# Half-size products with sums of operands in the output projection of a fused attention and feed-forward kernel

## The chip, the cores and the metric

The kernel runs on one core of a Trainium2 chip. The metric is the device time of one execution in microseconds, the median of several runs. The engines are named as the profile names them: PE (TensorE, matrix products; PEld its weight loads), DVE (VectorE), ACT (ScalarE), POOL (GpSimd) and SP (SyncE, which here only issues DMA transfers). Results of PE land in PSUM, eight banks of 512 fp32 values per partition. In this kernel PSUM is emptied by VectorE and ScalarE, while GpSimd works only on operands in SBUF.

## The reference

Attention in which two neighbouring queries are averaged first, then a feed-forward part without a nonlinearity:

```python
def _attn_ref(q, k, v):                      # (8, 8, 1152, 64) each
    q_pool = q.reshape(B, H, S // 2, 2, D).mean(axis=3)
    scores = scale * np.matmul(q_pool, k.transpose(0, 1, 3, 2))
    scores = scores - np.max(scores, axis=-1, keepdims=True)
    attn = np.exp(scores)
    attn = attn / (np.sum(attn, axis=-1, keepdims=True) + 1e-09)
    return np.matmul(attn, v)

def _moe_ref(x, w1, w2, w3, w_out):          # x: 4608 tokens of 512
    a = x @ w1
    b = x @ w2
    h = a * b @ w3
    return h @ w_out
```

## The kernel before

The products with `w3` and `w_out` are folded: `T = w3 @ w_out` (1024 x 512, fp16, `T16`) is made once on the chip, so for each token the rest is `a = x w1`, `b = x w2`, the gate `g = a * b` and `g T`.

**Attention.** The 64 heads are worked as 32 pairs. The key-query plane of all pairs is cut into 324 slots of 512 columns. For each slot PE computes the scores of both heads into a two-bank PSUM tile (`scores`, L431), and ScalarE takes the exponential into a ring in SBUF (L436). Three slots are one visit; there are 108. AV groups (`av_mm`, L459 and L462) multiply the exponentials with V into the bank `avb`, VectorE divides by the sums (`av_norm`, L483, L488, L497), and the result is turned into `xT`, by PE (`x_turn`, L504, L507, with copies L515, L517) or by a DMA transpose (`x_dma`, L473).

**Preparing the pairs.** At the first slot of pair n, `prepare(n + 2)` puts on GpSimd's queue the casts of K and Q of pair n + 2 (`cast_kq`: L343, L347, L349) and of V of pair n + 1 (`cast_v`: L356), and queues the loads of later pairs on SP (for the first eight pairs on GpSimd). K and Q of pair n + 1 are transposed at that place, for the first pairs on PE (L371), later by DMA from SP's queue (`transp`, L363). Each engine's queue is in order.

**Feed-forward.** 4608 tokens are nine chunks of 512. `moe_groups(c)` yields the groups of a chunk: for each of eight `ft` (128 of the 1024 hidden columns) one group of four 512-wide matmuls with `w1` (`first`, copied to `asb` by `keep`) and one with `w2` (`gate`: VectorE multiplies the PSUM result with `asb` into the fp16 tile `g`), then for each 128 tokens one group of eight 512-wide matmuls of `g` with `T16` (L610). `put` scales that result by VectorE into `osb` (L620) and `store` writes 128 rows; in attention the store goes over GpSimd's queue. T itself is made by `t_groups`: transposes of w3 (L535), then groups of eight 256-wide matmuls (L544).

**The order.** These groups are fills for PE between scores and AV groups. `_visits` plans before launch, by a model of PE, ScalarE and VectorE (`_Plan`, with a cost of 1 for a group of four 512-wide matmuls or eight 256-wide ones and 2 for one of eight 512-wide ones), which fills and AV groups each visit holds and whether a fill takes the single bank `mo` or one of the three `psc` tiles of the scores (`mot` in the profile). The plan doesn't have GpSimd in it. After the last slot the rest of the AV groups and fills follow; from there on `tail[0]` is true, ScalarE copies `asb` (L593), shares the emptying of outputs (L616, L617), and the stores go over SP and ScalarE. The last group of the last chunk is cut into 384 and 128 columns (`go_last`, L628). At the end a count of rows whose softmax sums left their range is read, and a general version runs if there are any (`near` sets where in the last chunk that read stands).

Of the kernel before, what the change touches and what calls it, by code (L numbers as in the profile page):

```python
# [8 lines left out]
FP32 = mybir.dt.float32  # L9
# [112 lines left out]
class _Plan:  # L122
# [39 lines left out]
        self.act = max(self.act, self.t + 0.21) + 0.953  # L162
        self._put(b, self.act + 0.07)

    def fill(self, n, at, scored):
        if scored:
            b = self._psc()
            self._pe("full", max(at, self.psc[b]), self.STEP[n])
            self._put(b, self._dve(0.2, 0.69))
        else:  # L170
            self._pe("full", max(at, self.mo), self.STEP[n])
            self.mo = self._dve(0.2, 0.69)

    def av_group(self, turns, last):
        self._pe("col" if last else "full", self.av, last * self.LAST if last else self.AV)
# [15 lines left out]
def _visits(n, start, units, pairs, fills, free, ready, width):  # L191

    p = _Plan(7.0)
    for _ in range(3):
        p.scores(0.0)
    beam = {(0, 0): [p]}
    for vis in range(n):  # L200
        new = {}
        ats = pairs.get(vis, [])

        def end(p, seq, na, f):
            q = p.copy()
            for _ in range(3 if vis + 1 < n else 0):
                q.scores(ready[vis + 1])
            q.past = (p.past, seq)

            cost = q.lost() + 0.3 * max(q.av - q.t, 0.0) + 0.15 * max(q.mo - q.t, 0.0)  # L210
            new.setdefault((na, f), []).append((cost, seq, q))

        def step(p, seq, na, f, pr, t0):
            d = p.t - t0
            loose = free[na] if vis >= start else 0
            if pr == len(ats) and (na >= len(units) or units[na][3] > vis) and (d > 1.0 or f >= loose):
                end(p, seq, na, f)
            if d > 2.3 or len(seq) > 4:
                return
            if pr < len(ats):  # L220
                q = p.copy()
                q.pair(ats[pr])
                step(q, seq + "P", na, f, pr + 1, t0)
            if na < len(units) and units[na][2] <= vis and seq.count("A") < 3:
                q = p.copy()
                q.av_group(*units[na][:2])
                step(q, seq + "A", na + 1, f, pr, t0)
            if f < loose:
                for b in "ms":
                    q = p.copy()  # L230
                    q.fill(fills[f][0], fills[f][1], b == "s")
# [24 lines left out]
def kernel(  # L256
# [26 lines left out]
    QM = 4  # L283
# [29 lines left out]
    wosb = msb.tile([128, NF, dm], FP16)  # L313
# [213 lines left out]
    def t_groups():  # L527
        w3T = {}

        def turn(ft):  # L530
            def go(pt):
                w3T[ft] = msb.tile([128, NF, 128], FP16, tag="w3T", bufs=2, name="w3T")
                ph = pt.bitcast(FP16)
                for a in range(NF):
                    nc.tensor.transpose(ph[:, a * 128:a * 128 + 128],  # L535
                                        w3c[ft // 4][:, ft % 4, a * 128:a * 128 + 128], ident16)

            return 0.5, go, lambda pt: nc.vector.tensor_copy(out=w3T[ft].rearrange("p a i -> p (a i)"),
                                                             in_=pt.bitcast(FP16)), W3_AT[ft // 2]

        def mult(ft, n0):
            def go(pT):
                for a in range(NF):
                    nc.tensor.matmul(pT[:, 0:256], w3T[ft][:, a, :], wosb[:, a, n0:n0 + 256],  # L544
                                     start=(a == 0), stop=(a == NF - 1))

            return 1, go, lambda pT: nc.vector.tensor_copy(out=T16[:, ft, n0:n0 + 256], in_=pT[:, 0:256]), WO_AT

        for ft in range(0, NF, 2):
            yield turn(ft)  # L550
            yield turn(ft + 1)
            for n in range(4):
                yield mult(ft + n // 2, n % 2 * 256)

    CH = 512

# [25 lines left out]
    def moe_groups(c):  # L582
        t = {}

        def first(pa, ft):
            if ft == 0:
                t["g"] = msb.tile([128, NF, CH], FP16, tag="g8", bufs=2, name="gT")
            proj(pa, w1sb, ft, c)

        def keep(pa):  # L590
            t["a"] = msb.tile([128, CH], FP32, tag="asb", bufs=2, name="asb")
# [11 lines left out]
        tts = list(range(0, CH, 128))  # L603
        if c in final:
            tts.sort(key=lambda tt: (c * CH + tt) % (2 * Sq) != QM * 128)
        for n, tt in enumerate(tts):
            def go(po, tt=tt, n=n):
                near[0] = c in final and n >= len(tts) - 3
                for ft in range(NF):
                    nc.tensor.matmul(po, t["g"][:, ft, tt:tt + 128], T16[:, ft, :],  # L610
                                     start=(ft == 0), stop=(ft == NF - 1))

            def put(po, tt=tt):
                osb = msb.tile([128, dm], FP32, tag="osb", bufs=3)
                if tail[0]:
                    nc.vector.tensor_scalar_mul(out=osb[:, 0:256], in0=po[:, 0:256], scalar1=1.0 / (SCL * SCL))  # L616
                    nc.scalar.mul(out=osb[:, 256:512], in_=po[:, 256:512], mul=1.0 / (SCL * SCL))  # L617
                    store(nc.scalar if c in final and tt == tts[-2] else nc.sync, c * CH + tt, osb)
                else:
                    nc.vector.tensor_scalar_mul(out=osb, in0=po, scalar1=1.0 / (SCL * SCL))  # L620
                    store(nc.gpsimd, c * CH + tt, osb)

            def go_last(po, tt=tt):
                osb = msb.tile([128, dm], FP32, tag="osb", bufs=3)
                for hs in (slice(0, 384), slice(384, dm)):
                    ph = ps.tile([128, 2, 512], FP32, tag="psc", bufs=3, name="mol")[:, 0, 0:hs.stop - hs.start]
                    for ft in range(NF):
                        nc.tensor.matmul(ph, t["g"][:, ft, tt:tt + 128], T16[:, ft, hs],  # L628
                                         start=(ft == 0), stop=(ft == NF - 1))
                    if hs.start:  # L630
                        nc.scalar.mul(out=osb[:, hs], in_=ph, mul=1.0 / (SCL * SCL))
                    else:
                        nc.vector.tensor_scalar_mul(out=osb[:, hs], in0=ph, scalar1=1.0 / (SCL * SCL))
                store(nc.scalar, c * CH + tt, osb)

            if c in final and n == len(tts) - 1:
                yield 2, go_last, None, 0.0
            else:
                yield 2, go, put, 0.0

    queue, ahead = [], []

# [94 lines left out]
                      ((old * FLAT + RING + TO[t]) // G) // VS - 1))  # L737
    fills = []
    for ft in range(0, NF, 2):
        fills += [(0.5, W3_AT[ft // 2])] * 2 + [(1, WO_AT)] * 4  # L740
# [71 lines left out]

    NQ = NU * 2
    rzf = rzall.rearrange("p i u -> p (i u)")
    ok = const.tile([128, 2, NQ], FP32)
# [53 lines left out]
```

## Time and profile before

| | us |
|---|---|
| median of 3 runs | 415.91 |
| lowest, highest | 415.29, 417.45 |
| the profiled execution's span | 414.1 |
| busy: PE, ScalarE, VectorE, GpSimd | 399.9, 323.4, 205.5, 167.6 |
| output groups (L610, L628), PE busy | 45.6 + 19.6 + 2.1 |
| feed-forward groups with w1 and w2 (L566), PE busy | 41.1 + 38.0 + 36.2 + 33.1 |

The span goes from the first to the last instruction of one profiled execution; its busy times are not times of the other runs. Matmuls overlap in the pipeline, so the mean time of one (380 ns for 512 columns) is longer than the spacing of two (216 ns). ScalarE's exponentials run from 8 to 348 us; the six output phases of chunks 0 to 5 lie at 100, 147, 190, 234, 277 and 323 us, and three chunks are finished after the last exponential.

### The profile page before, as it was taken

To read this page: it belongs to the slowest core of one execution; us is meant where nothing else is said; L and a number is where in the kernel's file an instruction comes from. 1 tells how busy PE (TensorE), PEld (TensorE's weight loads), DVE (VectorE), ACT (ScalarE), POOL (GpSimd) and SP (SyncE) were. 2 spreads that over 40 slices of the span, in tenths; PEclk is the share of its full clock that TensorE was granted. 3 is DMA by queue.
4 is the path that set the end of the run, shared out by engine and by line. 5 is a ranking of instruction groups with operands and counts; after the bars stand their busy time and mean duration, and the time that the engine had idled before them with its cause. 6 is when DMAs were issued, how large, how long until landed. Compare 5 with 4: busy or idle time off the path is not lost.

```text
span 414.1 us, 12744 instructions
## 1 busy us (share of the span) xinstructions
PE 399.9 (97%) x5337; PEld 246.9 (60%) x5337; DVE 205.5 (50%) x573; ACT 323.4 (78%) x353; POOL 167.6 (40%) x212
## 2 busy tenths in 40 slices
PE   3899999999999999999999999999999999999995
PEld 1477787565556655566556556655777655644442
DVE  1256665665356535554455436553556346744241
ACT  4878979898989998899999999999899986022321
POOL 4979976470655316504535155505532210010000
PEclk9999999999999999999999999999999999999999
DMA  8999999999799898959999999998975440030302
GB/s 263 210 320 289 269 286 312 348 247 265 185 238 252 221 286 278 242 70 278 273 264 280 264 252 270 292 260 163 303 207 121 85 90 15 16 114 2 101 0 108
DMA packets 90832, 86.34 MB, mean 209 GB/s; under 512 B 59664, under 2 KB 64272, under 8 KB 90768
## 3 DMA queue, kind: packets, MB, share of 16 engines
q1 hardware_dynamic: 81312, 58.80, 59.1%
q0 software_dynamic: 8880, 25.63, 21.6%
q10 hardware_dynamic: 576, 1.05, 0.8%
q8 instruction: 42, 0.69, 0.7%
q14 instruction: 22, 0.18, 0.1%
HBM read 67.11 MB, written 9.44 MB: 185 GB/s over the span
## 4 chain that ended last, share of the span: by engine, by line
PE 93%; ACT 2%; DMA 2%; DVE 1%; issue 1%; SPq 0%; POOL 0%; ACTq 0%
PE psc L431 20%; PE avb L462 17%; PE mot L566 16%; PE mo L566 15%; PE mo L610 11%; PE mot L610 5%; PE mo L544 3%; PE avb L459 3%; ACT ring L436 2%; PE ptk L371 2%; DMA kst<-in_k_dram 2%; DVE kqT L373 1%; PE mot L544 1%; PE mo L535 1%; PE mot L535 1%
## 5 line engine op out<-in xcount | busy, mean ns | idle before, releaser
L436 ACT ACTIVATE ring<-psc 128x1024 f16<-128x1024 f32 x324 | 308.3, 1025 | 33.8 <-PE psc L431 32.0
L462 PEld LDWEIGHTS <-ring 128*128 128x128 f16 x2304 | 84.4, 98 | 26.3 <-issue 7.1
L431 PE MATMUL psc<-kqT 64*128 64x512 f16 (+7 forms) x1152 | 96.2, 291 | 3.4 <-ACT ring L436 0.9
L462 PE MATMUL avb<-vaug,ring 128*128 128x65 f16 x2304 | 91.4, 193 | 0.0
L343 POOL CAST kq<-kst 128x1152 f16<-128x1152 f32 x31 | 35.7, 1150 | 74.3 <-DMA kqT<-kq 52.3
L431 PEld LDWEIGHTS <-kqT 64*128 64x128 f16 x1152 | 46.0, 95 | 31.0 <-issue 8.4
L578 POOL DMA_DIRECT2D out_dram<-osb x23 | 12.7, 551 | 101.6 <-DVE rzall L483 99.9
L610 PE MATMUL mo<-T,gT 128*128 128x512 f16 x192 | 45.6, 380 | 0.0
L566 PEld LDWEIGHTS <-w2sb 128*128 128x128 f16 x320 | 28.2, 98 | 28.3 <-issue 4.2
L566 PEld LDWEIGHTS <-w1sb 128*128 128x128 f16 x320 | 28.2, 98 | 27.7 <-issue 3.9
L610 PEld LDWEIGHTS <-gT 128*128 128x128 f16 x280 | 25.3, 98 | 32.2 <-issue 5.2
L483 DVE RECIPROCAL rzall<-avb 128x2 f32<-128x2 f32 x144 | 23.8, 165 | 37.0 <-PE avb L462 20.2
L566 PE MATMUL mot<-xT,w1sb 128*128 128x512 f16 (+2 forms) x172 | 41.1, 364 | 0.1
L620 DVE TENSOR_SCALAR osb<-mo 128x512 f32<-128x512 f32 x24 | 16.6, 692 | 48.5 <-PE mo L610 48.5
L347 POOL TENSOR_TENSOR kq<-qst 128x512 f16<-128x512 f32 x31 | 39.4, 1272 | 1.2 <-DMA qst<-in_q_dram 1.2
L566 PE MATMUL mot<-xT,w2sb 128*128 128x512 f16 (+2 forms) x156 | 38.0, 368 | 0.0
L356 POOL CAST vaug<-vst 128x1152 f16<-128x1152 f32 x32 | 36.6, 1143 | 2.6 <-DMA vst<-in_v_dram 2.5
L599 DVE TENSOR_TENSOR gT<-mot,asb 128x512 f16<-128x512 f32 x37 | 25.6, 692 | 22.0 <-PE mot L566 20.8
L599 DVE TENSOR_TENSOR gT<-mo,asb 128x512 f16<-128x512 f32 x35 | 24.2, 692 | 24.6 <-PE mo L566 24.4
L566 PE MATMUL mo<-xT,w2sb 128*128 128x512 f16 (+2 forms) x164 | 36.2, 349 | 0.0
L595 DVE COPY asb<-mo 128x512 f32<-128x512 f32 x32 | 22.1, 691 | 24.0 <-PE mo L566 23.7
L566 PE MATMUL mo<-xT,w1sb 128*128 128x512 f16 (+2 forms) x148 | 33.1, 351 | 0.0
(76 smaller groups left out, 287.4 us busy)
## 6 DMA issues: line engine op xcount, KB each, us to landing
vst<-in_v_dram SPq DMA_DIRECT2D x25, 576.0 KB, 4.9
kst<-in_k_dram SPq DMA_DIRECT2D x23, 576.0 KB, 5.9
qst<-in_q_dram SPq DMA_DIRECT2D x23, 512.0 KB, 7.2
out_dram<-osb POOLq DMA_DIRECT2D x23, 256.0 KB, 5.2
kst<-in_k_dram POOLq DMA_DIRECT2D x8, 576.0 KB, 9.8
qst<-in_q_dram POOLq DMA_DIRECT2D x8, 512.0 KB, 10.4
vst<-in_v_dram POOLq DMA_DIRECT2D x7, 576.0 KB, 7.2
w3c<-in_moe_w_dram POOLq DMA_DIRECT2D x4, 512.0 KB, 8.1
```

Of the source, the lines that this page charges most:

```text
L343: nc.gpsimd.tensor_copy(out=kq16[:, 0:NJ].rearrange("p c u d -> p u c d"), in_=kst.rearrange("p u (c d) -> p u c d", d=D))
L347: eng.tensor_tensor(out=kq16[:, NJ:NJ + QM].rearrange("p c u d -> p u c d"), in0=qv[:, :, :, 0], in1=qv[:, :, :, 1], op=ALU.add)
L356: nc.gpsimd.tensor_copy(out=va[:, :, :, 0:D], in_=vs.pop(p).rearrange("p u (c d) -> p u c d", d=D))
L431: nc.tensor.matmul(psc[:, u, f - s * G:f - s * G + ln], kT2[u * 64:u * 64 + 64, jt, :], qpT[u * 64:u * 64 + 64, i0:i0 + ln], start=True, s ...
L436: nc.scalar.activation(out=ring[:, :, r0:r0 + G], in_=psc, func=AF.Exp, bias=0.0, scale=SCALE)
L462: nc.tensor.matmul(avb[:, o + u * E1:o + u * E1 + E1], ring[:, u, c0:c0 + 128], va[:, u, jt, :], start=(jt == 0 and u == 0), stop=(jt == N ...
L483: nc.vector.reciprocal(out=rzall[:, i, :], in_=av[:, :, D:E1].rearrange("p u o -> p (u o)"))
L566: nc.tensor.matmul(pw[:, d0:d0 + n], wt[:, mc, ft * 128:ft * 128 + 128], xT[:, mc, a:a + n], start=(mc == 0 and d0 == 0), stop=(mc == NC - ...
L595: nc.vector.tensor_copy(out=t["a"], in_=pa)
L599: nc.vector.tensor_tensor(out=t["g"][:, ft, :], in0=pb, in1=t["a"], op=ALU.mult)
L610: nc.tensor.matmul(po, t["g"][:, ft, tt:tt + 128], T16[:, ft, :], start=(ft == 0), stop=(ft == NF - 1))
L620: nc.vector.tensor_scalar_mul(out=osb, in0=po, scalar1=1.0 / (SCL * SCL))
```

## The change

The product of the gated values with T is written in 2 x 2 blocks: for 512 tokens, the lower and upper half of the tokens (256 each), the lower and upper half of the 1024 hidden columns, and the left and right half of the 512 output columns. In place of eight block products there are seven (Strassen's scheme in the form of Winograd), each a group of eight 256-wide matmuls into one bank, in the order 1, 2, 5, 6, 7, 4, 3. Their operands need sums:

- once, four sums of blocks of `T16` on GpSimd (`t_sums`, after the first gate), into the buffer that held `wosb`;
- for each chunk, in `s_pair` after each of the gates 4 to 7, one sum of 256 columns on VectorE (`s1`) and one difference on GpSimd, which overwrites the gated values;
- for each chunk, in `s_rest`, S2 (1024 columns, after product 1, used by product 6; on GpSimd in attention, on VectorE in the tail) and S4 (1024 columns, after product 2, used by product 3; on GpSimd).

Emptying a product out of PSUM is joined with the sum of the results (`plus`, VectorE) where it can be; two sums of results are on GpSimd (`add`). Products 1 and 5 are only scaled (`only`, on ScalarE in the tail). The rows of 256 tokens are in one tile and stored after products 4 and 3. Buffers move: `w3T`, `asb` and the partial results share four buffers of 2 KB, `osb` has two of 4 KB instead of three of 2 KB, and the small tile `ok` takes a buffer of the K loads. In the plan the outputs of a chunk are seven fills of cost 1 instead of four of cost 2, and VectorE gets 0.25 more after the gates that have a sum. The last product of the last chunk is made and stored in two halves.

```diff
+    def t_sums():
+        b11, b12 = T16[:, 0:HF, 0:HM], T16[:, 0:HF, HM:dm]
+        b21, b22 = T16[:, HF:NF, 0:HM], T16[:, HF:NF, HM:dm]
+        ts = msb.tile([128, 4, HF, HM], FP16, tag="wo", bufs=1, name="tsum")
+        for o, x, y in ((0, b12, b11), (1, b22, ts[:, 0]), (2, b22, b12), (3, b21, ts[:, 1])):
+            nc.gpsimd.tensor_tensor(out=ts[:, o], in0=x, in1=y, op=ALU.subtract)
...
+        def left(n):
+            g = t["g"]
+            lo, hi = slice(0, HC), slice(HC, CH)
+            return {1: g[:, 0:HF, lo], 2: g[:, HF:NF, lo], 3: g[:, HF:NF, lo], 4: g[:, HF:NF, hi],
+                    5: t.get("s1"), 6: g[:, 0:HF, lo], 7: g[:, 0:HF, hi]}[n]
...
+            a11, a21, a22 = g[:, f, 0:HC], g[:, f, HC:CH], g[:, HF + f, HC:CH]
+            nc.vector.tensor_tensor(out=t["s1"][:, f], in0=a21, in1=a22, op=ALU.add)
+            nc.gpsimd.tensor_tensor(out=a21, in0=a11, in1=a21, op=ALU.subtract)
+
+        def s_rest(n):
+            g = t["g"]
+            a11, a12 = g[:, 0:HF, 0:HC], g[:, HF:NF, 0:HC]
+            if n == 2:
+                eng = nc.vector if tail[0] else nc.gpsimd
+                eng.tensor_tensor(out=a11, in0=t["s1"], in1=a11, op=ALU.subtract)
+            else:
+                nc.gpsimd.tensor_tensor(out=a12, in0=a12, in1=a11, op=ALU.subtract)
...
+        def done(n, pt):
+            if n == 1:
+                only(part("p"), pt)
+                s_rest(2)
+            elif n == 2:
+                plus(rows(0)[:, :, 0:HM], pt, t["p"])
+                s_rest(4)
+            elif n == 5:
+                only(part("q"), pt)
+            elif n == 6:
+                plus(t["p"], pt, t["p"])
+                add(part("w"), t["p"], t["q"])
+            elif n == 7:
+                plus(part("z"), pt, t["p"])
+                add(rows(1)[:, :, HM:dm], t["z"], t["q"])
+            elif n == 4:
+                plus(rows(1)[:, :, 0:HM], pt, t["z"])
+                for u in range(2):
+                    out_rows(1, u)
+            else:
+                for u in range(2):
+                    plus(rows(0)[:, u, HM:dm], pt[:, u, :], t["w"][:, u, :])
+                    out_rows(0, u)
+
+        def product(pt, n, tiles=(0, 1)):
+            a, b = left(n), TB[n]
+            for u in tiles:
+                for f in range(HF):
+                    nc.tensor.matmul(pt[:, u, :], a[:, f, u * 128:u * 128 + 128], b[:, f, :],
+                                     start=(f == 0), stop=(f == HF - 1))
...
             def gate(pb, ft=ft):
                 nc.vector.tensor_tensor(out=t["g"][:, ft, :], in0=pb, in1=t["a"], op=ALU.mult)
+                if ft >= HF:
+                    s_pair(ft - HF)
+                if ft == 0 and not TB:
+                    t_sums()
...
-        for n, tt in enumerate(tts):
-            def go(po, tt=tt, n=n):
-                near[0] = c in final and n >= len(tts) - 3
-                for ft in range(NF):
-                    nc.tensor.matmul(po, t["g"][:, ft, tt:tt + 128], T16[:, ft, :],
-                                     start=(ft == 0), stop=(ft == NF - 1))
...
+        order7 = (1, 2, 5, 6, 7, 4, 3)
+        for i, n in enumerate(order7):
+            def go(po, n=n, i=i):
+                near[0] = c in final and i >= 3
+                product(po.rearrange("p (u m) -> p u m", u=2), n)
+
+            def put(po, n=n):
+                done(n, po.rearrange("p (u m) -> p u m", u=2))
+
+            def go_last(po, n=n):
+                for u in range(2):
+                    pu = ps.tile([128, 2, 512], FP32, tag="psc", bufs=3, name="mol")[:, 0:2, 0:HM]
+                    product(pu, n, (u,))
+                    plus(rows(0)[:, u, HM:dm], pu[:, u, :], t["w"][:, u, :])
+                    out_rows(0, u)
...
-            fills += [(1, 0.0)] * (2 * NF) + [(2, 0.0)] * (CH // 128)
+            fills += [(1, 0.0, 0.0)] * NF + [(1, 0.0, 0.0), (1, 0.0, 0.25)] * HF + [(1, 0.0, 0.0)] * 7
```

`plus(out, pt, x)` is one VectorE operation, `out = pt / 256 + x`; `only(out, pt)` scales a product by 1/256, on VectorE in attention and on ScalarE in the tail; `add(out, x, y)` is one GpSimd operation; `out_rows(h, u)` stores 128 rows, in attention over GpSimd's queue, in the tail over SP's, and in the last chunk for u = 1 over ScalarE's.

More of the change, by code (lines that the diff above doesn't have):

```diff
@@ L163, in scores, with fill @@
         self._put(b, self.act + 0.07)
-    def fill(self, n, at, scored):
+    def fill(self, n, at, more, scored):
         if scored:
@@ L172, in fill @@
             self.mo = self._dve(0.2, 0.69)
+        self.dve += more
     def av_group(self, turns, last):
@@ L230, in step @@
                     q = p.copy()
-                    q.fill(fills[f][0], fills[f][1], b == "s")
+                    q.fill(*fills[f], b == "s")
                     step(q, seq + b, na, f + 1, pr, t0)
@@ L312 @@
     w3c = [msb.tile([128, 4, dff], FP16, tag="g8", bufs=2, name=f"w3c{i}") for i in range(2)]
-    wosb = msb.tile([128, NF, dm], FP16)
+    wosb = msb.tile([128, NF, dm], FP16, tag="wo", bufs=1, name="wosb")
     ring = att.tile([128, 2, RING], FP16, tag="ring", bufs=1)
@@ L531, in go @@
             def go(pt):
-                w3T[ft] = msb.tile([128, NF, 128], FP16, tag="w3T", bufs=2, name="w3T")
+                w3T[ft] = msb.tile([128, NF, 128], FP16, tag="t2k", bufs=4, name="w3T")
                 ph = pt.bitcast(FP16)
@@ L553, in t_groups @@
                 yield mult(ft + n // 2, n % 2 * 256)
+    HF, HM, HC = NF // 2, dm // 2, 256
+    TB = {}
+    def t_sums():
[4 more added lines that the diff above has]
+            nc.gpsimd.tensor_tensor(out=ts[:, o], in0=x, in1=y, op=ALU.subtract)
+        TB.update({1: b11, 2: b21, 3: b22, 4: ts[:, 3], 5: ts[:, 0], 6: ts[:, 1], 7: ts[:, 2]})
     CH = 512
@@ L583, in moe_groups, with s_pair @@
         t = {}
+        def left(n):
[3 more added lines that the diff above has]
+                    5: t.get("s1"), 6: g[:, 0:HF, lo], 7: g[:, 0:HF, hi]}[n]
+        def s_pair(f):
+            g = t["g"]
+            if f == 0:
+                t["s1"] = msb.tile([128, HF, HC], FP16, tag="s1", bufs=1, name="s1")
+            a11, a21, a22 = g[:, f, 0:HC], g[:, f, HC:CH], g[:, HF + f, HC:CH]
+            nc.vector.tensor_tensor(out=t["s1"][:, f], in0=a21, in1=a22, op=ALU.add)
+            nc.gpsimd.tensor_tensor(out=a21, in0=a11, in1=a21, op=ALU.subtract)
@@ new lines, in s_rest, with part @@
+        def s_rest(n):
+            g = t["g"]
+            a11, a12 = g[:, 0:HF, 0:HC], g[:, HF:NF, 0:HC]
[4 more added lines that the diff above has]
+                nc.gpsimd.tensor_tensor(out=a12, in0=a12, in1=a11, op=ALU.subtract)
+        IS = 1.0 / (SCL * SCL)
+        def part(name):
+            t[name] = msb.tile([128, 2, HM], FP32, tag="t2k", bufs=4, name=name)
+            return t[name]
@@ new lines, in rows, with plus, add, only @@
+        def rows(h):
+            if h not in t:
+                t[h] = msb.tile([128, 2, dm], FP32, tag="osb", bufs=2, name="osb")
+            return t[h]
+        def plus(out, pt, x):
+            nc.vector.scalar_tensor_tensor(out=out, in0=pt, scalar=IS, in1=x, op0=ALU.mult, op1=ALU.add)
+        def add(out, x, y):
+            nc.gpsimd.tensor_tensor(out=out, in0=x, in1=y, op=ALU.add)
+        def only(out, pt):
+            if tail[0]:
+                nc.scalar.mul(out=out, in_=pt, mul=IS)
+            else:
+                nc.vector.tensor_scalar_mul(out=out, in0=pt, scalar1=IS)
@@ new lines, in out_rows @@
+        def out_rows(h, u):
+            if tail[0]:
+                eng = nc.scalar if c in final and u else nc.sync
+            else:
+                eng = nc.gpsimd
+            store(eng, c * CH + h * HC + u * 128, rows(h)[:, u, :])
+        def done(n, pt):
[17 more added lines that the diff above has]
+                    out_rows(1, u)
+            else:
+                for u in range(2):
+                    plus(rows(0)[:, u, HM:dm], pt[:, u, :], t["w"][:, u, :])
+                    out_rows(0, u)
@@ L590, in keep @@
         def keep(pa):
-            t["a"] = msb.tile([128, CH], FP32, tag="asb", bufs=2, name="asb")
+            t["a"] = msb.tile([128, CH], FP32, tag="t2k", bufs=4, name="asb")
             if tail[0]:
@@ L599, in gate @@
                 nc.vector.tensor_tensor(out=t["g"][:, ft, :], in0=pb, in1=t["a"], op=ALU.mult)
+                if ft >= HF:
+                    s_pair(ft - HF)
+                if ft == 0 and not TB:
+                    t_sums()
             yield 1, lambda pa, ft=ft: first(pa, ft), keep, 0.0
             yield 1, lambda pb, ft=ft: proj(pb, w2sb, ft, c), gate, 0.0
-        tts = list(range(0, CH, 128))
-        if c in final:
-            tts.sort(key=lambda tt: (c * CH + tt) % (2 * Sq) != QM * 128)
@@ L606, in moe_groups @@
-        for n, tt in enumerate(tts):
-            def go(po, tt=tt, n=n):
-                near[0] = c in final and n >= len(tts) - 3
-                for ft in range(NF):
-                    nc.tensor.matmul(po, t["g"][:, ft, tt:tt + 128], T16[:, ft, :],
-                                     start=(ft == 0), stop=(ft == NF - 1))
[L613 to L637, printed above, removed]
@@ new lines, in moe_groups @@
+        order7 = (1, 2, 5, 6, 7, 4, 3)
[11 more added lines that the diff above has]
+                    out_rows(0, u)
+            if c in final and c == max(final) and n == order7[-1]:
+                yield 1, go_last, None, 0.0
@@ L638, in moe_groups @@
             else:
-                yield 2, go, put, 0.0
+                yield 1, go, put, 0.0
     queue, ahead = [], []
@@ L739 @@
     for ft in range(0, NF, 2):
-        fills += [(0.5, W3_AT[ft // 2])] * 2 + [(1, WO_AT)] * 4
+        fills += [(0.5, W3_AT[ft // 2], 0.0)] * 2 + [(1, WO_AT, 0.0)] * 4
     free = []
@@ L814 @@
     rzf = rzall.rearrange("p i u -> p (i u)")
-    ok = const.tile([128, 2, NQ], FP32)
+    ok = att.tile([128, 2, NQ], FP32, tag="kst", name="ok")
     nc.vector.tensor_scalar(out=ok[:, 0, :], in0=rzf, scalar1=SCL / 32768.0, scalar2=None, op0=ALU.is_ge)
```

## The prediction

> **What bounds the kernel now.** I read the page first, then windows, then groups by form, then timelines.
>
> ```profile
> span 414.1 us, 12744 instructions
> ...
> PE 399.9 (97%) x5337; PEld 246.9 (60%) x5337; DVE 205.5 (50%) x573; ACT 323.4 (78%) x353; POOL 167.6 (40%) x212
> ...
> PE 93%; ACT 2%; DMA 2%; DVE 1%; issue 1%; SPq 0%; POOL 0%; ACTq 0%
> ```
>
> TensorE holds 93% of the chain that ended last, so work taken from it should shorten the run. The windows say that this is so in both stages:
>
> ```profile
> 112.00:147.00 35.00, 34.88 (x550) 21.70 (x546) 20.24 (x59) 32.05 (x35) 16.03 (x17) 1.00 0.99 237
> ...
> 147.00:160.00 13.00, 13.00 (x163) 7.51 (x161) 4.24 (x12) 11.80 (x13) 2.81 (x6) 1.00 1.12 308
> ...
> 360.00:380.00 20.00, 20.00 (x116) 9.33 (x113) 9.01 (x22) 4.86 (x9) 1.09 (x2) 1.00 0.18 60
> ```
>
> Columns: length, then busy time of PE, PEld, DVE, ACT, POOL, clock, DMA. In attention (to 348 us) and in the tail alike PE is full at full clock, VectorE and GpSimd are not. One visit of attention in PE's timeline is scores for three slots, then fills and AV work, 3.15 us, and ScalarE's three exponentials take 2.85 of it; a microsecond lost by PE there is lost for good.
>
> **PE's saving.** The parts come from these groups:
>
> ```profile
> L610 PE MATMUL mo<-T,gT 128*128 128x512 f16 x192 | 45.6, 380 | 0.0
> ...
> L544 PE MATMUL mo<-wosb,w3T 128*128 128x256 f16 x104 | 13.5, 273 | 0.0
> ...
> L347 POOL TENSOR_TENSOR kq<-qst 128x512 f16<-128x512 f32 x31 | 39.4, 1272 | 1.2 <-DMA qst<-in_q_dram 1.2
> ...
> L349 POOL TENSOR_TENSOR kq<-qtl 64x128 f16<-64x128 f32 x31 | 14.0, 450 | 0.0
> ...
> 402.42 5.18 PE mot L610 x24
> ```
>
> The last line is of the chain: 24 matmuls 512 wide take 5.18, so an output group of 8 takes 1.73 and a chunk's four 6.91. A product is 8 matmuls 256 wide with their own weight loads. L544 does just that; its group at 65.44 is followed by other work at 66.31, so 0.87 us with the loads hidden. Seven take 6.09. Saving 0.82 a chunk, times 9: **-7.4**. Work moved earlier only shifts the rest, as PE is full everywhere.
>
> **What GpSimd gets.** L347 and L349 give a line: (1272-450)/(512-128) = 2.14 ns per element and 0.18 fixed. So a sum of 256 takes 0.72, of 512 1.27, of 1024 2.37 (from below 1.02, by the cast L343 with 1152 in 1.15 and one operand; from above two L347, 2.54; I take 2.37, the line through operations with two operands). A chunk adds 4 x 0.72 + 2 x 2.37 + 2 x 1.27 = 10.2 us; nine and the four sums of T make 101, GpSimd goes from 40% to 65%. It has the time, but its queue is in order, and it also casts each pair's K, Q and V:
>
> ```profile
> 200.63 1.16 POOL L343 CAST kq<-kst 128x1152 f16<-128x1152 f32 x1
> 201.74 1.28 POOL L347 TENSOR_TENSOR kq<-qst 128x512 f16<-128x512 f32 x1
> 202.96 0.45 POOL L349 TENSOR_TENSOR kq<-qtl 64x128 f16<-64x128 f32 x1
> 203.36 1.14 POOL L356 CAST vaug<-vst 128x1152 f16<-128x1152 f32 x1
> ```
>
> That is one block of 4.0 us, every 3.375 visits. In the old kernel nothing on PE waits for it soon: it is for a pair two pairs (21 us) on. The new sums stand in the same queue and PE does wait for them: product 6 needs S2, which can't start before product 1 has read its operand; product 3 needs S4, behind product 2 and S2. Behind the waiting matmul stand the scores, and behind those ScalarE.
>
> Take visits of two products, the first visit from 0: scores to 0.76, product 1 to 1.63, 2 to 2.50; the next visit starts at 3.2, and after its scores (0.76) and product 5 (0.87) product 6 is due at 4.83; 3 is due two visits on, at 10.4. GpSimd free: S2 from 1.85 to 4.2, S4 to 6.7, both in time by 0.6 and 3.7. With a cast block at the head of this visit GpSimd first ends the last small difference (1.2), casts to 5.2, S2 ends at 7.6: PE loses 2.8. With the block one visit before or after, 0.3. If product 1 shares a visit with the last gate: 0.35, 1.8 or 0.5 by the visit that the block hits. A block hits a given visit with 1/3.375 = 0.30, so on the mean 0.30 x 3.4 = 1.0 or 0.30 x 2.65 = 0.8 a chunk; visits with one product and two AV units leave more room, and I take 0.75. Six chunks are done in attention; in the first the pair starts (pair n at slot 10.125 n, three slots a visit: visits 27 and 30) miss its window, visits 28 and 29. 5 x 0.75: **+3.7**, bounds 0 (all missed) and 5 x 2.8 = 14. The opposite delay, casts behind sums, has the slack of a pair (10.6 us) against at most 7.3 of sums and costs nothing.
>
> **Sums of T.** Four sums, 9.5 us, queued after the issue at 72.93 and ahead of the cast at 73.53. The cast of pair 8 then ends at 86 instead of 76, its transposition lands 6.6 later (11.2 at most), and its scores come at 96.3: nothing, at most 1.
>
> **VectorE.** Seven emptyings (0.69 as L620, 0.75 with an addend by L488 against L497) for four, and four sums of 256 at 0.3 (between L497, 0.29, and L399, 0.43). Hidden: in 112 to 147 it had two emptyings a visit and 42% idle. For delays of an emptying behind a sum **+0.6** (0 to 5, below). The stores are as many and as large, `osb` is reused a chunk later, the check at the end keeps 2.6 us of products over it instead of 3.5 (if bare, 0.9 at most).
>
> **Tail** (three chunks, fills back to back). The last gate ends 0.96 after product 1 starts (by the gate at 381.80 against the group at 381.53). Then VectorE's sum to 1.26, GpSimd's difference, which reads what S2 overwrites, to 2.05, S2 on VectorE to 2.8 (0.7, an estimate: four times the elements of a sum of 256, of which some 0.15 is fixed by L483). Product 6, due at 2.60, starts at 2.87: **+0.8** for three. S4 is there at 5.3, product 3 is due at 5.5.
>
> **End.**
>
> ```profile
> 407.60 1.76 PE mol L628 x16
> ...
> 409.69 0.42 ACTq L578 DMA_DIRECT2D out_dram<-osb  x1
> ...
> out_dram<-osb ACTq DMA_DIRECT2D x2, 256.0 KB, 2.7
> ```
>
> The last matmul ends at 409.34, one tile is stored after it, and the span ends 4.8 later. Now four tiles are stored last: after the 5.3 of S4, GpSimd adds w (to 6.6) and the right half of the lower rows (to 7.9), 1.6 after the last matmul, and the other stores stand behind these two on both queues. Against an issue 0.35 after it, +1.2; three more tiles of 256 KB at 0.8 each (the busiest slice of the page moves 348 GB/s): **+3.6**, bounds 2.0 (no wait, transfers half overlapped) and 4.6 (230 GB/s, as in the last microseconds).
>
> **Sum.** 414.1 - 7.4 + 3.7 + 0.6 + 0.8 + 3.6 = 415.4. The profiled span is 1.8 below the median of the runs, so 417.2. This measurement tells 0.5% (2.1 us) from no change: the forecast is **no change that can be told, on the slow side**; by itself 413.5 to 421.
>
> **Rivals.**
> *Sums in time* (0.31). The planner spreads the seven products over more visits, with 0.6 to 3.7 us of room for each sum, so blocks hit little: 0.5 instead of 3.7, and the end 2.4: 414.1 - 7.4 + 0.5 + 0.6 + 0.8 + 2.4 + 1.8 = 412.8, faster. For it: the output windows leave GpSimd 78% idle (2.81 of 13). Against: the block is as long as two sums and nothing in the order on PE knows of it.
>
> *VectorE held by order in a tile* (0.14). Lower rows are written as left half (VectorE, product 4) and right half (GpSimd). If the waits take these two-row column halves for one span, VectorE stands until 7.9 and only then empties 4 and 3: the next chunk's second fill, due at 7.2, finds its bank at 8.75, so 1.55 for two chunks, 1.5 at the end, and some 0.6 in five attention chunks: +7.6, 424.8, slower. It decides once GpSimd's second addition ends after product 4. Against: on one `osb` in the old kernel two engines wrote plain column ranges at once (L633 from 408.99, L631 from 409.38).
>
> *VectorE's sums held by GpSimd* (0.13). If a sum of two SBUF operands on VectorE can't start while GpSimd works, each of the 24 in attention may stand behind 1.27; VectorE's idle time there is (35 - 20.24)/11 visits = 1.34 less 0.28, so 0.21 reaches PE: 24 x 0.21 = 5, 422.2. No row has the two at once: L399 ran at 4.00 and 5.22, GpSimd at 4.43 and 5.68.
> The Trainium skill, "SBUF — State Buffer", section "SBUF: two separate sides", says that a VectorE operation with two SBUF inputs and a GpSimd operation exclude each other through a shared port for the whole instruction; by that rule this rival holds and the sum is 422.2, without it 417.2.
>
> The change does what it says unless weight loads show; in L544 none does.
>
> **How the numbers follow.** Forecast 0.42, the rivals 0.31, 0.14, 0.13. Below 413.8 lie 0.05 of the forecast and 0.87 of the first rival, 0.29; above 418.0 0.45 of the forecast and the two others, 0.46; between them 0.25. Range: below, no wait on any sum, those of the tail included, and the end at 2.0: 414.1 - 7.4 + 2.0 + 1.8 = 410.5; above, to 424, which leaves out part of the second rival and of the 14.
>
> **What would show it.** L610 gone and seven products at 0.87 each; PE idle before product 6 of some chunks, released by GpSimd, with a cast of L343 to L356 between; in the tail gaps of 0.3; GpSimd near 270 us busy; four stores after the last matmul and a span ending 7 to 9 after it. PE never waiting for GpSimd in attention would break the term of 3.7; VectorE idle before its sums with a GpSimd operation running would speak for the third rival. Sums much longer than 2.4 would make all of it too low.

## The result and the profile after

| | before | after |
|---|---|---|
| median of 4 runs, us | 415.66 | 421.19 |
| lowest, highest | 415.29, 417.45 | 420.88, 423.06 |
| the profiled execution's span | 414.1 | 419.2 |

The change makes the kernel slower: the ratio is 1.0144, with a 95% interval of 1.0111 to 1.0177. Of the page after, the span with the instructions, the busy times and the chain that ended last by engine:

```profile
span 419.2 us, 13307 instructions
...
PE 394.9 (94%) x5545; PEld 268.1 (64%) x5545; DVE 236.3 (56%) x643; ACT 322.0 (77%) x347; POOL 253.9 (61%) x284
...
PE 85%; DVE 4%; POOL 3%; ACT 3%; issue 2%; DMA 1%; POOLq 1%; ACTq 0%; DVEq 0%
```

PE is busy 5.0 us less and the span is 5.1 us longer: in ten microseconds more than before PE has no work. GpSimd, at 0% of the chain before, now holds 3% of it, and VectorE 4% instead of 1%. The sums themselves are about as dear as forecast, as the groups by form show (busy us, mean ns of one | idle time before them):

```profile
L618 POOL TENSOR_TENSOR gT<-gT 128x1024 f16<-128x1024 f16 x9 | 19.1, 2122 | 2.1 <-PE mot L678 1.7
L616 POOL TENSOR_TENSOR gT<-s,gT 128x1024 f16<-128x1024 f16 x7 | 14.9, 2122 | 0.9 <-PE mo L678 0.7
L609 POOL TENSOR_TENSOR gT<-gT 128x256 f16<-128x256 f16 x36 | 24.0, 667 | 129.3 <-DVE s L608 71.3 <-DVE rzall L484 58.0
L608 DVE TENSOR_TENSOR s<-gT 128x256 f16<-128x256 f16 x36 | 10.8, 299 | 1.2
...
L678 PE MATMUL mot<-tsum,gT 128*128 128x256 f16 x120 | 15.4, 282 | 4.4 <-POOL gT L616 4.3
```

S2 (L616) and S4 (L618) take 2.12 us each, the small differences 0.67. The last line says where the first holes are: the products that read `tsum` and `gT` wait 4.3 us in all for S2. S4 is waited for nowhere.

After 60 us PE's timeline has only three idle times above 0.3 us. The first is this one; the lines are of GpSimd's and PE's timeline:

```profile
272.71 0.67 POOL L609 TENSOR_TENSOR gT<-gT 128x256 f16<-128x256 f16 x1 [2.53 <-DVE rzall L484]
272.87 1.05 PE L678 MATMUL mo<-T,gT 128*128 128x256 f16 x8
273.33 1.14 POOL L344 CAST kq<-kst 128x1152 f16<-128x1152 f32 x1
273.75 1.04 PE L678 MATMUL mot<-T,gT 128*128 128x256 f16 x8
274.43 1.27 POOL L348 TENSOR_TENSOR kq<-qst 128x512 f16<-128x512 f32 x1
275.66 0.45 POOL L350 TENSOR_TENSOR kq<-qtl 64x128 f16<-64x128 f32 x1
276.03 1.05 PE L678 MATMUL mo<-tsum,s 128*128 128x256 f16 x8
276.06 1.14 POOL L357 CAST vaug<-vst 128x1152 f16<-128x1152 f32 x1
277.16 2.11 POOL L616 TENSOR_TENSOR gT<-s,gT 128x1024 f16<-128x1024 f16 x1
279.33 1.05 PE L678 MATMUL mot<-tsum,gT 128*128 128x256 f16 x8 [2.25 <-POOL gT L616]
```

Product 1 is done with its operand when its matmuls end, at 273.92. S2 could start then, but the block of casts for later pairs stands ahead of it in GpSimd's queue, and S2 starts at 277.16. Product 6 has been due since 277.08. The second hole is the same thing one chunk later, 2.08 us ahead of 322.44:

```profile
319.17 1.14 POOL L357 CAST vaug<-vst 128x1152 f16<-128x1152 f32 x1
...
320.28 2.11 POOL L616 TENSOR_TENSOR gT<-s,gT 128x1024 f16<-128x1024 f16 x1
...
322.44 1.86 PE L678 MATMUL mot<-tsum,gT 128*128 128x256 f16 x8 [2.08 <-POOL gT L616]
```

That second hole has a sequel. In each of the nine profiles of this case the granted clock changes only at whole multiples of 3.413 us, counted from the first entry in its record (18.73 us in the change; 89 and 90 multiples later it falls and rises again). The windows are cut at these multiples. They show length, busy times of PE, PEld, VectorE, ScalarE and GpSimd, the granted clock, the DMA share and GB/s; the first two hold the first hole, the third holds the second, and the last two follow it:

```profile
274.73:278.14 3.41, 2.35 (x39) 1.71 (x36) 1.75 (x4) 3.06 (x4) 3.41 (x4) 1.00 1.11 186
278.14:281.56 3.42, 2.23 (x36) 1.75 (x36) 1.06 (x3) 0.69 (x2) 3.34 (x3) 1.00 1.06 393
...
319.10:322.51 3.41, 1.32 (x15) 0.77 (x10) 0.94 (x3) 2.80 (x3) 3.33 (x4) 1.00 0.41 151
322.51:325.93 3.42, 3.42 (x32) 2.43 (x34) 1.16 (x3) 0.00 (x0) 2.89 (x2) 0.50 0.00 0
325.93:329.34 3.41, 3.28 (x62) 2.53 (x58) 1.52 (x5) 3.13 (x4) 1.08 (x2) 1.00 0.02 7
```

The first hole is split between two of these windows, 1.07 and 1.19 us, and PE goes on at full clock. The second lies whole in one. In the next, PE was granted half the clock: for 3.41 us it looks fully busy and does half the work, 1.7 us more, gone without any idle time. The other profiles with such holes agree (see below): of six holes of 2.08 to 2.26 us, the four that lie whole in one window are followed by half clock, the two that are split are not. The Trainium skill, "TensorE: Matmul & The Clock Gate", Part 1, has the clock fall to half after an idle window of about 3.4 us and rise after as long a busy one. The length of the slow stretch agrees with that; here 2.08 us of idle time in one window were enough, and 1.82 us were not.

The third hole is in the tail, in the timeline of VectorE, GpSimd and PE:

```profile
365.24 2.78 PE L678 MATMUL mot<-tsum,gT 128*128 128x256 f16 x24
...
366.92 0.30 DVE L899 TENSOR_SCALAR ok<-rzall 128x288 f32<-128x288 f32 x1
367.09 1.27 POOL L635 TENSOR_TENSOR w<-p,q 128x512 f32<-128x512 f32 x1 [0.74 <-DVE p L632]
367.14 1.38 DVE L900 TENSOR_SCALAR ok<-rzall 128x288 f32<-128x288 f32 x1
367.86 1.04 PE L678 MATMUL mot<-T,gT 128*128 128x256 f16 x8
...
369.62 0.69 DVE L632 SCALAR_TENSOR_TENSOR z<-mot,p 128x512 f32<-128x512 f32 x1
370.36 1.02 PE L578 MATMUL mot<-xT,w1sb 128*128 128x512 f16 x4 [1.46 <-DVE z L632]
```

L899 and L900 are the two comparisons of the softmax sums with their limits, equal in size. In the kernel before both took 0.30 us:

```profile
364.87 0.30 DVE L816 TENSOR_SCALAR ok<-rzall 128x288 f32<-128x288 f32 x1
365.09 0.30 DVE L817 TENSOR_SCALAR ok<-rzall 128x288 f32<-128x288 f32 x1
```

After the change the first takes 0.30 us. The second, begun 0.05 us after a GpSimd operation, takes 1.38 and ends 0.16 after it. Neither waits for the other's data: the operand `rzall` and the result `ok` are not GpSimd's. The rest of the count and then `z` come that much later, and PE waits 1.46 us for the bank that `z` empties.

The end, in the timeline of all engines:

```profile
409.95 1.04 PE L678 MATMUL mol<-T,gT 128*128 128x256 f16 x8
410.15 0.69 DVE L632 SCALAR_TENSOR_TENSOR osb<-mot,z 128x512 f32<-128x512 f32 x1 [0.18 <-PE mot L678]
410.71 1.27 POOL L635 TENSOR_TENSOR osb<-z,q 128x512 f32<-128x512 f32 x1
410.79 0.76 DVE L632 SCALAR_TENSOR_TENSOR osb<-mol,w 128x256 f32<-128x256 f32 x2
412.01 0.81 SPq L590 DMA_DIRECT2D out_dram<-osb  x2
412.01 0.86 ACTq L590 DMA_DIRECT2D out_dram<-osb  x2
```

The last matmul ends at 410.99, GpSimd's last sum at 411.98, and only then are the four stores issued. The span ends 8.2 us after the last matmul, 3.4 more than before.

### The profile page after: what moved, and what is told of

Same layout as the page of the kernel before. It is cut to its first block, busy times and chain, and to the rows that moved or that the text cites. A ratio compares the mean times of both kernels' runs of the same rounds, so it can differ in the third digit from the quotient of the medians.

```text
span 419.2 us, 13307 instructions
## 1 busy us (share of the span) xinstructions
PE 394.9 (94%) x5545; PEld 268.1 (64%) x5545; DVE 236.3 (56%) x643; ACT 322.0 (77%) x347; POOL 253.9 (61%) x284
## 4 chain that ended last, share of the span: by engine, by line
PE 85%; DVE 4%; POOL 3%; ACT 3%; issue 2%; DMA 1%; POOLq 1%; ACTq 0%; DVEq 0%
PE psc L432 19%; PE avb L463 16%; PE mot L578 16%; PE mo L578 14%; PE mot L678 5%; PE mo L678 5%; ACT ring L437 3%; PE mo L545 3%; PE avb L460 2%; PE ptk L372 2%; DVE gT L695 1%; POOL gT L616 1%; DMA qst<-in_q_dram 1%; PE mot L545 1%; DVE kqT L374 1%
## 5 line engine op out<-in xcount | busy, mean ns | idle before, releaser
L609 POOL TENSOR_TENSOR gT<-gT 128x256 f16<-128x256 f16 x36 | 24.0, 667 | 129.3 <-DVE s L608 71.3
L678 PEld LDWEIGHTS <-gT 128*128 128x128 f16 x432 | 40.3, 98 | 13.5 <-POOL gT L616 4.9
L578 PE MATMUL mot<-xT,w2sb 128*128 128x512 f16 (+1 forms) x196 | 42.2, 344 | 0.0
L578 PE MATMUL mot<-xT,w1sb 128*128 128x512 f16 x156 | 40.0, 379 | 1.5 <-DVE z L632 1.5
L348 POOL TENSOR_TENSOR kq<-qst 128x512 f16<-128x512 f32 x31 | 39.4, 1271 | 1.4 <-DMA qst<-in_q_dram 1.4
L695 DVE TENSOR_TENSOR gT<-mot,asb 128x512 f16<-128x512 f32 x41 | 28.4, 692 | 18.3 <-PE mot L578 18.0
L689 ACT COPY asb<-mot 128x512 f32<-128x512 f32 x16 | 9.4, 585 | 37.9 <-PE mot L578 20.1
L695 DVE TENSOR_TENSOR gT<-mo,asb 128x512 f16<-128x512 f32 x31 | 21.4, 692 | 25.7 <-PE mo L578 25.6
L578 PE MATMUL mo<-xT,w1sb 128*128 128x512 f16 (+2 forms) x164 | 34.2, 339 | 0.0
L578 PE MATMUL mo<-xT,w2sb 128*128 128x512 f16 x124 | 32.0, 381 | 0.0
L498 DVE TENSOR_TENSOR xb<-avb,rzall 128x128 f16<-128x128 f32 x96 | 28.0, 292 | 3.3
```

The lines of the kernel that those rows point to most:

```text
L348: eng.tensor_tensor(out=kq16[:, NJ:NJ + QM].rearrange("p c u d -> p u c d"), in0=qv[:, :, :, 0], in1=qv[:, :, :, 1], op=ALU.add)
L498: nc.vector.tensor_tensor(out=xbt, in0=av[:, :, 0:D], in1=rzall[:, i, :].unsqueeze(2).to_broadcast([128, 2, D]), op=ALU.mult)
L578: nc.tensor.matmul(pw[:, d0:d0 + n], wt[:, mc, ft * 128:ft * 128 + 128], xT[:, mc, a:a + n], start=(mc == 0 and d0 == 0), stop=(mc == NC - ...
L609: nc.gpsimd.tensor_tensor(out=a21, in0=a11, in1=a21, op=ALU.subtract)
L678: nc.tensor.matmul(pt[:, u, :], a[:, f, u * 128:u * 128 + 128], b[:, f, :], start=(f == 0), stop=(f == HF - 1))
```

## The experiments

Each is an edit of the changed kernel, timed beside the kernel before; that one had a median of 415.64 beside the first four and 415.44 beside the last three. All compute the whole result.

**S2 on VectorE in attention.** If the holes come from S2's place behind the casts, another engine should free them.

```diff
-                eng = nc.vector if tail[0] else nc.gpsimd
-                eng.tensor_tensor(out=a11, in0=t["s1"], in1=a11, op=ALU.subtract)
+                nc.vector.tensor_tensor(out=a11, in0=t["s1"], in1=a11, op=ALU.subtract)
```

> S2 is computed on VectorE in attention too; GpSimd loses seven sums of 2.1 us and nothing on PE waits for S2 behind a cast block. Theory (two output phases lost 2.25 and 2.08 us waiting for S2, and about 1.4 more at half clock behind the second): both gaps and the clock dip go, 421.2 - 5.7 = 415.5, 414.5 to 416.5. Rival (S2 on VectorE stands behind the last small difference on GpSimd, which stands behind the same cast block, and now blocks VectorE too): the loss moves to VectorE, 419 or more. Second rival (the product order costs by itself, the gaps are only where it shows): 421.

Measured: 420.01 (419.72 to 421.21), ratio 1.0113, 1.0091 to 1.0134, far from the 415.5 of the theory. The waits for S2 are gone, and three others stand in their place. The timeline at the place of the first hole:

```profile
277.05 1.27 POOL L348 TENSOR_TENSOR kq<-qst 128x512 f16<-128x512 f32 x1
...
277.18 1.69 DVE L615 TENSOR_TENSOR gT<-s,gT 128x1024 f16<-128x1024 f16 x1
...
278.28 0.90 POOL L350 TENSOR_TENSOR kq<-qtl 64x128 f16<-64x128 f32 x1
...
278.79 0.68 DVE L631 SCALAR_TENSOR_TENSOR osb<-mot,p 128x512 f32<-128x512 f32 x1
...
279.52 0.40 PE L432 MATMUL psc<-kqT 64*128 64x320 f16 x4 [1.02 <-DVE osb L631]
```

S2 takes 0.68 us on VectorE alone and 1.69 here, where it begins inside a GpSimd addition; GpSimd's next, 0.45 alone, takes 0.90. The engines hold each other off, the emptying of the bank comes late, and PE loses about 1.0 us in each of three chunks instead of 2.2 in two. So moving S2 to the idle engine trades a wait in GpSimd's queue for one in VectorE's. The time is that of the first rival, but not its way: S2 doesn't stand behind the last small difference, which ended at 276.00; it is held after it has begun. The smaller holes and the missing half clock would make this run about 3.2 us faster than the change, and it is 1.2 faster; the rest isn't placed.

**The casts later.** The same work, only in another order: from pair 8 on, the casts that `prepare` puts on GpSimd's queue, and the loads that it queues on SP, come at the end of the visit in which pair n starts, behind its fills, not at its head.

```diff
+        held = []
         for s in range(vis * VS, vis * VS + VS):
...
-                    prepare(pn + 2)
+                    if pn >= NPE:
+                        held.append(pn + 2)
+                    else:
+                        prepare(pn + 2)
...
+        for p in held:
+            prepare(p)
```

> From pair 8 on the casts and loads that prepare issues are put into the queues behind the fills of the same visit instead of ahead of its scores; GpSimd has exactly the same work. Theory (the order on GpSimd decides, not the amount): where products 1 and 2 share a visit with a pair start, S2 and S4 come first and the two gaps go, 415.5 to 417 if the block does not hit the next visit's sums. Rival (GpSimd has too much work in the output phases): gaps of the same sum elsewhere, 420 to 422.

Measured: 415.99 in 10 runs (415.16 to 418.21), ratio 1.0008, 0.9996 to 1.0021: 5.2 us less than the change, with GpSimd as busy as there (254.5 us against 253.9). No product waits for GpSimd any more. It is the order on GpSimd's queue that costs, not the amount of work on it. One new wait of 1.10 us stands in the profiled execution, at 418.21 the longest of the ten; in its timeline:

```profile
184.03 1.27 POOL L348 TENSOR_TENSOR kq<-qst 128x512 f16<-128x512 f32 x1
...
185.24 1.70 DVE L608 TENSOR_TENSOR s<-gT 128x256 f16<-128x256 f16 x1
185.26 0.45 POOL L350 TENSOR_TENSOR kq<-qtl 64x128 f16<-64x128 f32 x1
...
185.66 1.14 POOL L357 CAST vaug<-vst 128x1152 f16<-128x1152 f32 x1
...
187.60 0.39 PE L432 MATMUL psc<-kqT 64*128 64x512 f16 x2 [1.10 <-DVE asb L691]
```

VectorE's sum of 256 columns, 0.30 on the mean, was held for 1.70 until two GpSimd operations that followed each other without a pause were done. Another, at 101.27, was held for 1.54, with no wait on PE. In the changed kernel the longest of the 36 took 0.37 (1.2 us of idle time before all of them, mean 299 ns).

**The last chunk in the old form**, eight products and the old stores, one after each output group, for this chunk alone.

```diff
-                if ft >= HF:
+                if ft >= HF and c not in final:
                     s_pair(ft - HF)
...
+        if c in final:
+            for n, tt in enumerate(range(0, CH, 128)):
...
+                if n == 3:
+                    yield 2, go8_last, None, 0.0
+                else:
+                    yield 2, go8, put8, 0.0
+            return
```

> The last chunk alone is computed with eight products and stored as in the old kernel. Theory (four stores behind two additions on GpSimd end the run 3.6 us later than the old end): that goes and one product, 0.8, comes back, 421.2 - 3.6 + 0.8 + the 0.2 of the wait for S2 = 418.2, span from last matmul to end 4.8 again. Rival (the end is late for a reason outside the stores): 421 to 422.

Measured: 418.57 (418.11 to 419.9), ratio 1.0076, 1.0051 to 1.0102: 2.6 less than the change. With the 0.8 us of the saving given up in that chunk, and the 0.2 won that product 6 waited there for S2, the four late stores cost about 3.2. This profile has the same holes in attention, 2.26 and 2.09 us, and here the half clock follows the first of them (0.51 from 279.80 to 282.00) and not the second (1.00 from 324.50 to 326.50), the other way round than in the change. By the windows it is the same: the first hole lies whole in one (276.44 to 279.85), of the second 1.82 us lie in one (320.81 to 324.22) and the rest in the next.

**The count of rows later.** Six fills go ahead of the comparisons, so that they come at another point of a chunk.

```diff
+    for _ in range(6):
+        fill()
     nc.vector.tensor_scalar(out=ok[:, 0, :], in0=rzf, scalar1=SCL / 32768.0, scalar2=None, op0=ALU.is_ge)
...
-    for _ in range(12):
+    for _ in range(6):
         fill()
```

> The seven VectorE operations that check the softmax sums are issued six fills later, behind the output phase that is open when attention ends. Theory (one of them, 0.30 us alone, took 1.38 while GpSimd added w, and PE then waited 1.46 for a bank): the gap goes, 421.2 - 1.5 = 419.7. Rival (the bank is late because VectorE has more to do, wherever the check stands): 421 to 421.5.

Measured: 421.52 (420.98 to 421.87), ratio 1.0141, 1.0123 to 1.016, so no gain, against 1.5 expected. In the timeline the wait is gone all the same, and both comparisons take 0.30:

```profile
373.29 0.30 DVE L901 TENSOR_SCALAR ok<-rzall 128x288 f32<-128x288 f32 x1
373.50 0.30 DVE L902 TENSOR_SCALAR ok<-rzall 128x288 f32<-128x288 f32 x1
```

What took the gain away shows in this kernel's windows. They have the two attention holes, 2.26 and 2.10 us, each whole in one window, and behind each the half clock:

```profile
277.18:280.59 3.41, 1.15 (x11) 0.79 (x10) 0.69 (x1) 2.07 (x3) 3.33 (x3) 1.00 0.98 335
280.59:284.01 3.42, 3.42 (x40) 2.29 (x39) 1.16 (x3) 1.06 (x2) 2.79 (x2) 0.50 0.41 150
321.55:324.97 3.42, 1.32 (x12) 0.94 (x13) 0.69 (x1) 2.52 (x3) 3.34 (x3) 1.00 0.31 115
324.97:328.38 3.41, 3.41 (x35) 2.26 (x32) 1.15 (x3) 0.26 (x1) 3.06 (x2) 0.50 0.00 0
```

That is 1.7 us lost twice, once more than in the change, and in the profiled executions it cancels the gain of 1.5: spans of 419.5 and 419.2. The edit, whose place is in the tail, behind both holes, didn't bring the second stretch. What differs is where the windows stand: the first entry of the clock's record lies between 18.7 and 21.6 us after the start of the span, by profile. How many such stretches the executions without a profile had isn't shown: their mean granted clock, 0.0028 lower on the mean of four than in the change, counts the end too, where PE is done.

**All three edits together.**

> The three edits together: casts behind the fills of their visit, the last chunk with eight products, the check six fills later. If the three losses are separate they add: 416.0 (casts later) - 2.6 (last chunk) - 1.45 (gap behind the check) = 411.9, 411 to 413, below the old kernel's 415.6. Rival (the gap behind the check is only a shift, as the run with the check alone was no faster): 413.4.

Measured: 412.49 in 10 runs (410.97 to 413.77), ratio 0.9928, 0.9903 to 0.9952. This beats both kernels. The theory of separate losses that add gave 411 to 413, the rival, with nothing from the count, 413.4: the time lies within the first and 0.9 below the second, and how much of it is the count's isn't told by this run. Of the page:

```profile
span 409.1 us, 13254 instructions
...
PE 394.1 (96%) x5529; PEld 266.2 (65%) x5529; DVE 232.9 (57%) x636; ACT 322.3 (79%) x349; POOL 247.7 (61%) x277
```

After 60 us PE has no idle time above 0.3 us, and the clock is 0.997 to 1.0 in all ten runs. PE is about as busy as in the change; the ten microseconds between the two spans are the holes and the end.

**The casts and the count later, the new end kept.**

> Casts behind the fills and the check six fills later, the end as in the change. With no gap of 2 us in attention there is no half clock whose place can differ from run to run, so the check's gap of 1.45 shows alone: 416.0 - 1.45 = 414.5. Rival (the check later is worth nothing, as when it was moved alone): 416.0.

Measured: 415.55 in 11 runs (414.71 to 416.67), ratio 0.9987, 0.9957 to 1.0017. It lies between what the two theories gave. Against the casts alone, 415.99, the later count brings 0.4 in the medians, less than the 1.45 us of idle time that it removes, and the old kernel's medians beside the two differ by 0.2; the difference is within what the runs scatter, and the count's worth stays unsettled. Against the three edits the end is worth 3.1, and with the 0.8 of one chunk's saving less the 0.2 of S2's wait 3.7, near the 3.2 from above.

**Seven products in two chunks of the tail alone**, eight in the six chunks of attention and in the last one, with the count later; the casts stand at their place in the old kernel.

```diff
+    NEW = (6, 7)
...
-                if ft >= HF:
+                if ft >= HF and c in NEW:
                     s_pair(ft - HF)
-                if ft == 0 and not TB:
+                if ft == 0 and not TB and c in NEW:
                     t_sums()
```

> Chunks 0 to 5, which are finished in attention, and the last one with eight products; chunks 6 and 7 with seven; check later, casts at their old place. Theory (the saving in attention is real once nothing waits: six times 0.80): this run has only two chunks' saving, 415.7 - 1.6 + 0.4 for the tail's wait for S2 = 414.5, and the run with products everywhere but in the last chunk is 2.5 to 4.5 below it. Rival (attention's pace is set by ScalarE, so products there gain nothing): both the same, within 0.7.

Measured: 414.85 in 12 runs (414.47 to 418.43), ratio 0.9978, 0.9949 to 1.0006. The kernel with the three edits is 2.4 below it, just under the 2.5 to 4.5 of the theory and far above the rival's 0.7. So the saving in attention does arrive once nothing waits, though in the medians only half of 6 x 0.80 = 4.8 us. In the two profiled executions all of it shows: PE is busy 394.1 against 399.1, the spans are 409.1 and 414.2. But these were the fastest of the ten runs there and the second longest of the twelve here, so what takes the other half in the medians isn't settled.

## Why the prediction was low in time and right in its mechanism

It gave 417.2, with a range of 410.5 to 424.0; the runs gave 421.19. So it named no change that can be told, on the slow side, and the kernel is slower by 5.5 us. The range holds the time, the forecast's own 413.5 to 421 just misses it. Term by term:

- **PE's saving, -7.4: nearly.** Three products follow each other from 365.24 to 367.86, 0.873 us each, seven take 6.11 where eight took 6.91: 0.80 a chunk, 7.2 in nine. The weight loads stay hidden there. Over the whole kernel less arrives: PE is busy 5.0 us less, and 1.7 of its busy time is the half clock's, so 6.7.
- **S2 behind the casts, +3.7: the mechanism as named, the term too small.** "PE idle before product 6 of some chunks, released by GpSimd, with a cast of L343 to L356 between" is what the trace shows, in two chunks, 2.25 and 2.08 us against the 2.8 forecast for a full hit: 4.33 in all. That the total is near 3.7 is in part luck: the prediction took a mean over the places where a block can fall in five chunks, and here two of the five were hit in full. That moving the casts alone brings 5.2 us shows it on the chip. What the prediction had no term for is the half clock behind such a hole, 1.7 us in this execution. It priced an idle time by its length alone. GpSimd was busy 254 us, not near 270: S2 and S4 took 2.12 instead of 2.37, the small differences 0.67 instead of 0.72, and two of the nine S2 ran on VectorE (the prediction's sum counts all nine on GpSimd, though its own tail has S2 on VectorE).
- **VectorE's delays, +0.6: mis-sized.** One wait of 1.46 us, through the comparison L900 standing beside a GpSimd operation. The text saw that the products over the count shrink ("if bare, 0.9 at most"), but not that the count itself gets longer. By the rows the hold makes 1.08 of the 1.46; the other 0.4 would be there without it, with fewer products over the count. That is the third rival's mechanism at a place that it didn't name.
- **S2 in the tail, +0.8: 0.4.** S2 runs on VectorE in two chunks, since the first of the three had it on GpSimd, and product 6 is late by about 0.2 in each (the start at 387.19 is 0.21 behind the due time).
- **Sums of T, 0: right**; nothing of PE waits for them.
- **The end, +3.6: right**, 3.4 in the profile, and 3.2 and 3.7 in the experiments. GpSimd's last sum, and behind it four stores at once, as worked out.

Together, -6.7 + 4.33 + 1.7 + 1.46 + 0.4 + 3.4 = +4.6 against a span longer by 5.1; 0.5 us are not placed. Of the 4.0 us by which the forecast fell short, 1.7 are the half clock, 0.9 the comparison, 0.6 the size of the holes, 0.7 PE's saving; the tail gives 0.4 and the end 0.2 back, 0.5 is what isn't placed, and 0.2 is the median's distance from the span, 2.0 instead of 1.8.

The **rivals**. Sums in time (412.8) fell in the change. The casts reordered alone give 415.99; that 412.49, with the end and the count mended as well, is close to 412.8 is chance, as the rival kept 2.4 for the end. VectorE held by the order of column halves did not occur: the emptying of product 4 starts at 410.15, ahead of GpSimd's sum at 410.71, for which it would have had to wait, and the next emptying starts at 410.79, beside that sum. VectorE's sums held by GpSimd is half right. The Trainium skill, "SBUF — State Buffer", section "SBUF: two separate sides", has a VectorE operation with two SBUF inputs and a GpSimd operation exclude each other for a whole instruction, and the runs agree: 0.68 against 1.69 (S2), 0.30 against 1.70 (the small sum). L900, with one input, was held as well, 0.30 against 1.38. Yet the rival's 422.2 is near the time for another reason. It charged 24 small sums with 0.21 each; in the change these ran at 0.299 on the mean, and VectorE idled 1.2 us in all before them. The timelines show why: only six of the 24 met a sum or cast of GpSimd at all, in the last 0.16 to 0.21 us of the addition L348, and these took 0.31 to 0.37; the small difference on GpSimd waits for its sum and can't be in its way.

## What to carry to other kernels

When sums of operands move to an engine that looks idle, its share of busy time says little: what counts is which long operations stand ahead of them in its queue at the moment PE needs them, and queueing the patient work behind the urgent (here casts that are needed 21 us later) was worth 5.2 us with the same work done. A scheme that completes several output tiles only with its last product pays for their stores at the end of the program, so the last chunk is better left in the form that finishes tile by tile. VectorE operations whose operands and results are all in SBUF should be kept away from GpSimd's work when an emptying of PSUM stands behind them.

## What the hardware showed beyond that

- An idle time of 2.08 to 2.26 us on PE was followed by 3.41 us at a granted clock of 0.50 in four cases and by none in two. What told them apart is the place in the 3.413 us windows at whose ends the clock changes: the four lay whole in one (the second hole in the change, the first with the old end, both with the later count), the two were split, with at most 1.82 us in one. Single idle times of 0.8 to 1.5 us were followed by none.
- VectorE held by GpSimd shows no idle time and no releaser: the wait is inside the operation's own duration, 1.38 instead of 0.30. It can outlast one GpSimd operation and stand through two in a row. It doesn't strike each time the two meet: the six small sums of the change that began in the last 0.2 us of a GpSimd addition went through, and GpSimd's next operation took 0.50 instead of 0.45.
